# A top-k attention and GELU kernel: two weight units converted ahead of the first slot, and a reordered start

## The chip, the cores and the metric

The kernel runs on one NeuronCore of a Trainium2 chip. The core has five engines that run side by side, each with its own queue in order: TensorE (PE, matrix products), VectorE (DVE), ScalarE (ACT), GpSimd (POOL) and SyncE (SP, which here only issues transfers). The metric is the time of one execution on the device in microseconds (us), the median of several runs.

## The reference

Attention over 8 batches and 8 heads, 576 rows of 64, in which each row of scores keeps its 32 largest values; then a two-layer MLP with an exact GELU over the 4608 resulting rows of 512.

```python
scores = scale * np.matmul(q, k.transpose(0, 1, 3, 2))        # (8, 8, 576, 576)
kth = np.partition(scores, -32, axis=-1)[..., -32:-31]
scores = np.where(scores >= kth, scores, -1e9)
attn = np.exp(scores - scores.max(-1, keepdims=True))
attn = attn / (attn.sum(-1, keepdims=True) + 1e-09)
x = np.matmul(attn, v)  # heads joined: (4608, 512)
h = x @ w_in            # (4608, 2048)
g = 0.5 * h * (1.0 + erf(h / sqrt(2)))
out = g @ w_out         # (4608, 512)
```

q, k and v arrive as 4-byte floats, w_in and w_out as 8-byte floats. The kernel computes in 4-byte floats, so the weights have to be converted on the chip.

## The kernel before

**Attention.** Two heads of a batch form a pair (32 pairs). Their 576 rows are cut into four blocks of 128 and a rest of 64; the rests of two pairs make one item. There are 144 items, in an order that takes, in the first batch, blocks 0 and 1 of all four pairs first (items 0 to 7), then blocks 2 and 3. For a pair, PE transposes q and k in three pieces (`transpose_qk`, L220), and ACT (for the very first pair partly DVE) copies them out of PSUM. For an item, `scores` (L263) multiplies into two PSUM tiles, `s_ps` (one buffer) and `t_ps` (two buffers under the tag `tp`, shared with all transposes), and ACT evicts them, scaled, in L281 and L282 (L303 and L304 for rests). `top_k` (L309) finds the 32nd value of each row on DVE with eight MAX8 and six MATCH_REPLACE8 per item. `threshold` (L334) is two small POOL instructions. `softmax` (L358) is two ACT instructions per head; `add_small` (L352, POOL) and `inverse` (L346, DVE, L350) make the reciprocal of its sum; `normalise` (L369, L376) multiplies by it, one instruction per head, on POOL or DVE. `transposes` (L384) and `attend` (L426, products L444) give 256 columns of x.

**The MLP.** `l1_piece` (L496) and `l2_piece` (L532) are blocks of products, in a fixed list; `mlp(n)` takes up to n from it, as long as the rows of x that they need are there. GELU runs on ACT (L507), after a load of its table.

**The slots.** The loop at L617 runs over n, one slot per item; everything is put into each engine's queue in the order in which it is written. Slot n holds, in this order: the POOL part of a weight unit (`weights_add`), scores of item n + 2, the product of x for item n - 3, pieces of the MLP, the transposes of item n - 2, the softmax of item n - 1, the q and k transposes of a pair to come, top-k of item n (with `inverse(n - 1)` at its end on DVE), the threshold of item n, `normalise(n - 1)`, the ACT part of the next slot's unit (`weights_size`), the loads of the unit two slots on (`load_weights`), and in the first slots a load of v. Item 7 (`HASTE`) is different: its normalisation is put into the middle of the next top-k, on DVE, so that the MLP can begin in slot 9. The load of the q and k of a later pair is issued by SP when the last piece of a pair has been transposed.

**The weights.** They are cut into 16 units of 256 rows by 512 columns. A unit's 8-byte words are loaded by SP in two transfers (L160), to a part of `w_out_sb` that isn't yet in use, or to an extra tile `words`. ACT makes parts of the result with three instructions (L175, L177, L179; for units of slot 9 and later, `on_pool`, POOL does the third, L191), and POOL adds them up in two (L194, L195). Unit number i of `ORDER` has slot i + 1 (the last one i + 2), so slots 1 to 15 and 17. In a slot before one with a unit, `normalise` has one of its two instructions on DVE, or both if that unit is `on_pool`; without a unit both are on POOL.

**The start.** Memsets on POOL clear the rest blocks of the tiles for k and q, DVE that of the first v tile; POOL makes the identity matrix for the transposes. k of pair 0 is loaded by ACT's queue and its last 64 rows by POOL's; q and everything else by SP's. 16 products of zeros (L596, `WARM`) keep PE occupied until k is there. Then come the transposes of pair 0, the scores of items 0 and 1, and the transposes of pair 1, all ahead of slot 0.

Of the kernel before, what the change touches and what calls it, by code (L numbers as in the profile page):

```python
# [14 lines left out]
def kernel(  # L15
# [19 lines left out]
    nc = tc.nc  # L35
# [34 lines left out]

    raws = {n: [const.tile([P, NJ, 2, D], f32, name=f"raw_{n}{i}") for i in range(m)]
            for n, m in (("k", 2), ("q", 2), ("v", NP + 1))}
    for n, ts in raws.items():
        for t in ts[: 1 if n == "v" else 2]:
            (nc.vector if n == "v" else nc.gpsimd).memset(t[:, NM], 0.0)
    make_identity(nc, ident)
    for t in raws["v"][1:]:
        nc.gpsimd.memset(t[:, NM], 0.0)


    n_pairs = B * NP
# [5 lines left out]
    def load(n, pair, queue=None, queue2=None):  # L87
        if pair >= n_pairs:
            return
        queue = queue or nc.sync  # L90
        queue2 = queue2 or queue
        b, h0 = pair // NP, 2 * (pair % NP)
        t, src = raw_of(n, pair), sources[n]
        for e in range(2):
            queue.dma_start(
                out=t[:, 0:NM, e, :], in_=src[b, h0 + e, 0:SM].rearrange("(t p) d -> p t d", p=P)
            )
            queue2.dma_start(out=t[e * TL : (e + 1) * TL, NM, e, :], in_=src[b, h0 + e, SM:S])

# [18 lines left out]


    ORDER = [0, 1, 2, 3, 8, 9, 4, 5, 10, 11, 6, 7, 12, 13, 14, 15]
    FIRST = 1
    START = 2 * NP + 1
    HASTE = 2 * NP - 1
    WARM = 16
    words = {}
    low = const.tile([P, 1], f32, name="low")
    nc.gpsimd.memset(low, -EXP0 * 2.0**19)
# [1 line left out]
    nc.gpsimd.memset(high, EXP0 * 2.0**-21)  # L131


    SLOT_OF = {u: FIRST + i + (i == UNITS - 1) for i, u in enumerate(ORDER)}
    UNIT_IN = {n: u for u, n in SLOT_OF.items()}
    unit_in = UNIT_IN.get

    def load_weights(n, queue=None):

        queue = queue or nc.sync  # L140
        u = unit_in(n)
        if u is None:
            return
        src, r, c, dst = weights_of(u)
        if src.dtype == f32:
            for x in range(2):
                queue.dma_start(
                    out=dst[:, x], in_=src[(r + x) * P : (r + x + 1) * P, c : c + WS]
                )
            return  # L150


        half, i = src.bitcast(u16), ORDER.index(u)
        if i not in (12, 14, 15):
            at = FT // 2 + 4 * (i % 2)
            t = w_out_sb[:, at : at + 4, :].rearrange("p (a b) n -> p a (b n)", a=2)
        else:
            t = stage.tile([P, 2, 2 * WS], f32, tag="words", name="words")
        for a in range(2):
            queue.dma_start(  # L160
                out=t[:, a].bitcast(u16)[:, 0 : 4 * WS - 1],
                in_=half[(r + a) * P : (r + a + 1) * P, 4 * c + 1 : 4 * (c + WS)],
            )
        words[u] = t
# [16 lines left out]
    def on_pool(u):  # L181

        return SLOT_OF[u] >= START

    made = set()

    def weights_add(u):
        if u in words:
            w, _, below, d = parts(u)
            if on_pool(u):  # L190
                nc.gpsimd.tensor_scalar(  # L191
                    w.bitcast(i32), w.bitcast(u32), 2.0**-13, None, op0=ALU.mult
                )
            nc.gpsimd.tensor_tensor(d, d, below, op=ALU.add)  # L194
            nc.gpsimd.tensor_tensor(d, d, w.bitcast(i32), op=ALU.add)  # L195
        made.add(u)
# [53 lines left out]
    def spread(t, step, n):  # L250

        return bass.AP(tensor=t.tensor, offset=t.offset, ap=[list(t.ap[0]), [step, 2], [1, n]])
# [10 lines left out]
    def scores(i):  # L263
        if i >= N:
            return
        pair, t = items[i]
        S_of[i] = s = work.tile([P, 2 * S], f32, tag="s", bufs=5, name="s")
        s_ps = ps.tile([P, 2, 512], f32, tag="s", bufs=1, name="s_ps")
        t_ps = ps.tile([P, 512], f32, tag="tp", name="t_ps")
        if t < NM:  # L270
            qk = qk_of[pair]
            lhsT = qk[:, t * P : (t + 1) * P]
            nc.tensor.matmul(t_ps[:, 0:P], lhsT=lhsT, rhs=qk[:, SM + P : KT], start=True, stop=True)  # L273
            for c in range(2):
                for e in range(2):
                    rows = slice(e * D, (e + 1) * D)
                    nc.tensor.matmul(  # L277
                        s_ps[:, e, c * 256 : (c + 1) * 256], lhsT=lhsT[rows, :],
                        rhs=qk[rows, KT + c * 256 : KT + (c + 1) * 256], start=True, stop=True,
                    )  # L280
            nc.scalar.activation(spread(s, S + TL, SM), s_ps, func=AF.Copy, scale=scale)  # L281
            nc.scalar.activation(s[:, SM : S + TL], t_ps[:, 0:P], func=AF.Copy, scale=scale)  # L282
        else:
            for r in range(2):
                qk = qk_of[pair + r]
                for e in range(2):
                    nc.tensor.matmul(  # L287
                        t_ps[half(r, e), r * TL : (r + 1) * TL],
                        lhsT=qk[:, SM + e * TL : SM + (e + 1) * TL],
                        rhs=qk[:, SM + P + e * TL : SM + P + (e + 1) * TL],  # L290
                        start=True, stop=True,
                    )

            for r in range(2):
                qk = qk_of[pair + r]
                for e in range(2):
                    rows = slice(e * D, (e + 1) * D)
                    nc.tensor.matmul(  # L298
                        s_ps[half(r, e), r, :], lhsT=qk[rows, SM + e * TL : SM + (e + 1) * TL],
                        rhs=qk[rows, KT:], start=True, stop=True,  # L300
                    )
            s2 = s.rearrange("p (r n) -> p r n", r=2)
            nc.scalar.activation(s2[:, :, 0:SM], s_ps, func=AF.Copy, scale=scale)  # L303
            nc.scalar.activation(  # L304
                s2[:, :, SM:S], t_ps[:, 0:P].rearrange("p (r n) -> p r n", r=2),
                func=AF.Copy, scale=scale,
            )
# [274 lines left out]
    staging = ExitStack()  # L582
    stage = staging.enter_context(tc.tile_pool(name="stage", bufs=1))

    load("k", 0, nc.scalar, nc.gpsimd)
    load("q", 0)
    load("k", 1)
    load("q", 1)
    for n in range(2):
        load_weights(FIRST + n)  # L590


    idle = raws["v"][0][:, NM].rearrange("p e d -> p (e d)")
# [3 lines left out]
    for pair in range(2):  # L597
        for piece in transpose_qk(pair, pair == 0):
            piece()
        if pair == 0:  # L600
            scores(0)
            scores(1)

# [11 lines left out]
    for n in range(ahead):  # L617

        left[0] = 7 if START < n < START + 2 * NP else 8
        weights_add(unit_in(n))  # L620
        scores(n + 2)

        product = attend(HASTE) if n - 2 == HASTE else n - 3 != HASTE and attend(n - 3)
        late = n > START
        mlp(1)
        tr = transposes(n - 2) if n - 2 != HASTE else []
        if product and n > START and done[0] < len(pieces) and pieces[done[0]][0] > ready[0]:

            for piece in tr[:1]:
                piece()  # L630
            tr, ready[0] = tr[1:], n_tok[0]
        softmax(n - 1, 0)
        mlp(1)
        if not late:
            softmax(n - 1, 1)
        mlp(1)
        prep = prep_in.pop(n, [])
        if len(prep) > 1 and len(tr) == 3:
            tr, prep = tr[:1] + prep[:1] + tr[1:], prep[1:]
        for piece in tr[:-1]:  # L640
            piece()
            ready[0] = n_tok[0]
            mlp(1)
        ready[0] = n_tok[0]
        if late:
            softmax(n - 1, 1)
        if n - 1 != HASTE:
            add_small(n - 1)
        for piece in tr[-1:] + prep:
            piece()  # L650
            mlp(1)

        run_gelus()
        mlp(left[0])
        run_gelus()
        if n - 1 == HASTE:

            def hasty():
                st = stat_of[HASTE]
                nc.vector.tensor_scalar(st["den"], st["den"], 1e-9, None, op0=ALU.add)  # L660
                inverse(HASTE)
                normalise(HASTE, 2)

            top_k(n, {1: hasty})
            for piece in transposes(HASTE):
                piece()
        elif n < N:
            top_k(n, {3: lambda: inverse(n - 1)})
        else:
            inverse(n - 1)  # L670
        threshold(n)
        u = unit_in(n + 1)

        if n - 1 != HASTE:
            normalise(n - 1, 0 if u not in words else 2 if on_pool(u) else 1)

        weights_size(unit_in(n + 1))
        if n >= FIRST:
            load_weights(n + 2)
        if n <= NP:  # L680
            load("v", n)

# [37 lines left out]
```

## Time and profile before

| | |
|---|---|
| median of 4 runs | 1652.29 us (1651.49 to 1652.75) |
| the profiled execution: time | 1651.49 us |
| its span, first to last instruction | 1649.7 us |
| mean granted clock of PE | 0.979 |
| busy: PE, DVE, ACT, POOL | 1591.3, 1420.7, 1183.5, 651.2 us |
| first top-k instruction on DVE | 11.59 us after the start of the span |
| first product of the MLP (L496) | 109.1 us |
| bytes moved | 56.14 MB |

The span starts with the first instruction and ends with the last; the time of the run is a little longer. Busy times of the engines overlap. A line of the profile that names a group of instructions has the line of the kernel, the engine, the operation, output and inputs, how many there were, the busy time and the mean of one, and then how long the engine stood idle before them and what released it. Where a line says `PE tp L413 <- ACT s L304`, PE's instruction of line 413 waited for ACT's of line 304. The granted clock is the share of full speed at which TensorE was allowed to run.

### The profile page before, as it was taken

What the parts mean: (1) busy time and instruction counts of PE and PEld (TensorE: products, weight loads), DVE (VectorE), ACT (ScalarE), POOL (GpSimd) and SP (SyncE); (2) the same over time, 40 slices, a digit from 0 to 9 for tenths busy, and PEclk for the clock granted to TensorE, in tenths of its full rate; (3) what the DMA queues carried; (4) which work ended last, traced back from release to release, by engine and by line L of the source; (5) the groups of instructions that cost most, each with busy time, mean ns of one, the idle gap of its engine ahead of it and who ended that gap; (6) DMA issues with size and microseconds to landing.
All of it is one profiled execution on the core that took longest, in us unless ns stands there. A gap on an engine that the chain in (4) does not pass through costs nothing.

```text
span 1649.7 us, 25054 instructions
## 1 busy us (share of the span) xinstructions
PE 1591.3 (96%) x8832; PEld 1078.9 (65%) x8832; DVE 1420.7 (86%) x3051; ACT 1183.5 (72%) x2130; POOL 651.2 (39%) x755
## 2 busy tenths in 40 slices
PE   5679799999999999999999999999999999999999
PEld 4355576766666667676666667676666666666665
DVE  7999899988899889998989988998889888999800
ACT  6889867777777777777777777777777777777720
POOL 3778633333333333333333333333333333333300
PEclk7789899999999999999999999999999999999999
DMA  6424210011101111011100111001110001000000
GB/s 174 140 90 131 55 43 1 14 29 33 46 1 28 30 30 28 1 28 36 30 28 5 38 30 43 1 14 28 44 35 1 27 16 35 2 13 6 2 13 13
DMA packets 126621, 56.14 MB, mean 34 GB/s; under 512 B 117760, under 2 KB 117792, under 8 KB 126496
## 3 DMA queue, kind: packets, MB, share of 16 engines
q1 hardware_dynamic: 125376, 54.25, 12.3%
q8 instruction: 70, 1.15, 0.3%
q14 instruction: 55, 0.45, 0.1%
q10 hardware_dynamic: 1056, 0.26, 0.1%
q0 software_dynamic: 64, 0.03, 0.0%
HBM read 45.08 MB, written 9.44 MB: 33 GB/s over the span
## 4 chain that ended last, share of the span: by engine, by line
PE 92%; ACT 4%; DVE 3%; issue 1%; POOL 0%; ACTq 0%; POOLq 0%
PE h_ps L496 30%; PE y_ps L532 30%; PE o L444 9%; PE s_ps L277 8%; PE tp L413 7%; PE tp_qk L232 2%; DVE top L324 2%; PE t_ps L273 2%; DVE rest L327 1%; PE o L455 1%; PE s_ps L298 1%; PE tp_t L395 1%; ACT s L364 1%; ACT s L363 1%; PE t_ps L287 0%
## 5 line engine op out<-in xcount | busy, mean ns | idle before, releaser
L324 DVE MAX8 top<-rest 128x8 f32<-128x576 f32 x864 | 609.3, 747 | 0.0
L496 PE MATMUL h_ps<-xT,w_in_sb 128*128 128x256 f32 (+1 forms) x2560 | 553.8, 361 | 3.8 <-ACT g L507 3.8
L532 PE MATMUL y_ps<-w_out_sb,g 128*128 128x512 f32 x1152 | 549.4, 599 | 0.0
L496 PEld LDWEIGHTS h_ps<-xT,w_in_sb 128*128 128x128 f32 x2560 | 429.5, 191 | 67.4 <-issue 19.7
L376 POOL TENSOR_SCALAR s<-s,rden 128x576 f32<-128x576 f32 x265 | 454.3, 1723 | 0.4 <-DVE rden L350 0.4
L327 DVE MATCH_REPLACE8 rest<-top,rest 128x576 f32<-128x576 f32 x576 | 423.3, 742 | 0.0
L356 POOL TENSOR_SCALAR den<-den 128x2 f32<-128x2 f32 x143 | 31.7, 222 | 832.5 <-ACT s L364 831.9
L532 PEld LDWEIGHTS y_ps<-w_out_sb,g 128*128 128x128 f32 x1152 | 195.0, 190 | 166.1 <-issue 164.9
L281 ACT ACTIVATE s<-s_ps 128x1024 f32<-128x1024 f32 x128 | 131.5, 1028 | 168.1 <-PE s_ps L277 146.3
L364 ACT ACTIVATE s<-s,bias 128x576 f32<-128x576 f32 x288 | 223.3, 775 | 12.7
L363 ACT ACTIVATE s<-s,neg 128x576 f32<-128x576 f32 x288 | 224.1, 778 | 0.3 <-POOL neg L339 0.2
L413 PEld LDWEIGHTS tp<-ident,s 128*128 128x128 f32 x1152 | 146.6, 145 | 116.0 <-issue 58.9
L420 ACT COPY pt<-tp 128x512 f32<-128x512 f32 x256 | 147.1, 574 | 102.7 <-PE tp L413 102.6
L327 DVE MATCH_REPLACE8 rest<-top,s 128x576 f32<-128x576 f32 x288 | 211.7, 742 | 0.0
L413 PE MATMUL tp<-ident,s 128*128 128x128 f32 x1152 | 180.0, 281 | 27.8 <-ACT pt L396 20.0
L324 DVE MAX8 top<-s 128x8 f32<-128x576 f32 x288 | 201.8, 742 | 3.9 <-ACT s L282 3.9
L444 PE MATMUL o<-pt,raw_v 128*64 128x256 f32 x1280 | 155.8, 391 | 0.0
L277 PE MATMUL s_ps<-qk 64*128 64x256 f32 x1024 | 151.5, 416 | 0.7 <-ACT s L281 0.7
L350 DVE RECIPROCAL rden<-den 128x2 f32<-128x2 f32 x144 | 23.0, 160 | 138.2 <-POOL den L356 137.9
L444 PEld LDWEIGHTS o<-pt,raw_v 128*64 128x64 f32 x1280 | 87.8, 139 | 66.5 <-issue 24.6
L277 PEld LDWEIGHTS s_ps<-qk 64*128 64x128 f32 x1024 | 91.6, 193 | 23.5 <-issue 1.6
L507 ACT ACTIVATE g<-h_ps 128x512 f32<-128x512 f32 x144 | 78.6, 595 | 33.7 <-PE h_ps L496 32.9
(67 smaller groups left out, 1088.3 us busy)
## 6 DMA issues: line engine op xcount, KB each, us to landing
raw_q<-in_q_dram SPq DMA_DIRECT2D x64, 128.0 KB, 2.4
raw_v<-in_v_dram SPq DMA_DIRECT2D x64, 128.0 KB, 2.5
out_dram<-y SPq DMA_DIRECT2D x32, 256.0 KB, 2.2
w_out_sb<-in_moe_w_in_dram SPq DMA_DIRECT2D x16, 511.8 KB, 4.9
raw_k<-in_k_dram SPq DMA_DIRECT2D x62, 128.0 KB, 2.5
w_out_sb<-in_moe_w_out_dram SPq DMA_DIRECT2D x10, 511.8 KB, 4.1
words<-in_moe_w_out_dram SPq DMA_DIRECT2D x6, 511.8 KB, 4.5
raw_q<-in_q_dram SPq DMA_DIRECT2D x64, 16.0 KB, 2.2
```

The source lines that it names most:

```text
L277: nc.tensor.matmul(s_ps[:, e, c * 256 : (c + 1) * 256], lhsT=lhsT[rows, :], rhs=qk[rows, KT + c * 256 : KT + (c + 1) * 256], start=True, s ...
L281: nc.scalar.activation(spread(s, S + TL, SM), s_ps, func=AF.Copy, scale=scale)
L324: nc.vector.max(st["top"][:, e, 8 * r : 8 * r + 8], cur[e])
L327: nc.vector.match_replace(rest[:, e], st["top"][:, e, 8 * r : 8 * r + 8], cur[e], LOWEST)
L363: nc.scalar.activation(s, s, func=AF.Prelu, bias=st["neg"][:, e, 1:2], scale=1.0, alpha=STEEP)
L364: nc.scalar.activation(s, s, func=AF.Exp, bias=st["bias"][:, e : e + 1], scale=1.0, accum_out=st["den"][:, e : e + 1],)
L376: (nc.vector if e >= 2 - on_dve else nc.gpsimd).tensor_scalar(s, s, st["rden"][:, e : e + 1], None, op0=ALU.mult)
L413: nc.tensor.transpose(tp[:, j * P : (j + 1) * P], s[:, first + j * P : first + (j + 1) * P], ident)
L420: nc.scalar.copy(out=dst, in_=tp.rearrange("p (j n) -> p j n", j=NM))
L444: nc.tensor.matmul(o[e * D : (e + 1) * D, 0:n], lhsT=vt[:, j, e, :], rhs=pt[:, e * NM + j if j < NM else 2 * NM, :], start=(j == 0), stop= ...
L496: nc.tensor.matmul(h_tile(u)[:, i, :], lhsT=w_in_sb[:, ko, f * P : (f + 1) * P], rhs=xT[:, ko, c0 : c0 + n], start=(ko == 0), stop=(ko == ...
L532: nc.tensor.matmul(y_of[sub], lhsT=g_of[u][:, i, sub * P : (sub + 1) * P], rhs=w_out_sb[:, f, :], start=(f == 0), stop=(f == FT - 1),)
```

## The change

1. The first two units have slot 0: their ACT part is put ahead of the loop, behind the transposes of pair 1. All later units move two slots ahead, to slots 1 to 13 and 15. Three units instead of two are loaded ahead of the loop, and the third one's words go to the extra tile.
2. The memsets are redistributed: POOL clears only the first k tile, DVE the others. The loads of pair 0 are issued ahead of the identity matrix, so POOL issues k's last rows as its second task.
3. Nine products of zeros in place of 16.
4. The scores of item 0 are evicted in three instructions: ACT takes the first head's 512 columns, DVE the 128 of the rest and the second head's 512.

What follows from 1: the number of units that are `on_pool` goes from eight to six, and slots 13 and 16 have no unit's ACT part any more, so their `normalise` is on POOL.

```diff
-    for n, ts in raws.items():
-        for t in ts[: 1 if n == "v" else 2]:
-            (nc.vector if n == "v" else nc.gpsimd).memset(t[:, NM], 0.0)
-    make_identity(nc, ident)
-    for t in raws["v"][1:]:
-        nc.gpsimd.memset(t[:, NM], 0.0)
+    nc.gpsimd.memset(raws["k"][0][:, NM], 0.0)
+    for t in raws["v"][:1] + raws["q"] + raws["k"][1:] + raws["v"][1:]:
+        nc.vector.memset(t[:, NM], 0.0)
...
+    load("k", 0, nc.scalar, nc.gpsimd)
+    load("q", 0)
+    make_identity(nc, ident)
...
-    WARM = 16
+    WARM = 9
...
-    SLOT_OF = {u: FIRST + i + (i == UNITS - 1) for i, u in enumerate(ORDER)}
+    SLOT_OF = {u: max(0, i - 1) + (i == UNITS - 1) for i, u in enumerate(ORDER)}
+    def units_in(n):
+        return [u for u in ORDER if SLOT_OF[u] == n]
...
-        if i not in (12, 14, 15):
+        if i not in (2, 12, 14, 15):
...
+            if i == 0:
+                nc.scalar.activation(s[:, 0:SM], s_ps[:, 0], func=AF.Copy, scale=scale)
+                nc.vector.tensor_scalar(s[:, SM : S + TL], t_ps[:, 0:P], scale, None, op0=ALU.mult)
+                nc.vector.tensor_scalar(s[:, S + TL :], s_ps[:, 1], scale, None, op0=ALU.mult)
+                return
...
-    load("k", 0, nc.scalar, nc.gpsimd)
-    load("q", 0)
     load("k", 1)
     load("q", 1)
-    for n in range(2):
-        load_weights(FIRST + n)
+    for u in units_in(0) + units_in(1):
+        load_weights(u)
...
+    for u in units_in(0):
+        weights_size(u)
...
-        weights_add(unit_in(n))
+        for u in units_in(n):
+            weights_add(u)
...
-            normalise(n - 1, 0 if u not in words else 2 if on_pool(u) else 1)
-
-        weights_size(unit_in(n + 1))
-        if n >= FIRST:
-            load_weights(n + 2)
+            normalise(n - 1, 0 if not us else 2 if on_pool(us[0]) else 1)
+        for u in us:
+            weights_size(u)
+        for u in units_in(n + 2):
+            load_weights(u)
```

More of the change, by code (lines that the diff above doesn't have):

```diff
@@ L122 @@
     ORDER = [0, 1, 2, 3, 8, 9, 4, 5, 10, 11, 6, 7, 12, 13, 14, 15]
-    FIRST = 1
     START = 2 * NP + 1
     HASTE = 2 * NP - 1
-    WARM = 16
+    WARM = 9
     words = {}
@@ L131, with load_weights @@
     nc.gpsimd.memset(high, EXP0 * 2.0**-21)
-    SLOT_OF = {u: FIRST + i + (i == UNITS - 1) for i, u in enumerate(ORDER)}
[L135 to L143, printed above, removed]
+    SLOT_OF = {u: max(0, i - 1) + (i == UNITS - 1) for i, u in enumerate(ORDER)}
+    def units_in(n):
+        return [u for u in ORDER if SLOT_OF[u] == n]
+    def load_weights(u):
+        queue = nc.sync
         src, r, c, dst = weights_of(u)
@@ L671 @@
         threshold(n)
-        u = unit_in(n + 1)
+        us = units_in(n + 1)
         if n - 1 != HASTE:
-            normalise(n - 1, 0 if u not in words else 2 if on_pool(u) else 1)
-        weights_size(unit_in(n + 1))
-        if n >= FIRST:
-            load_weights(n + 2)
+            normalise(n - 1, 0 if not us else 2 if on_pool(us[0]) else 1)
[3 more added lines that the diff above has]
+            load_weights(u)
         if n <= NP:
```

## The prediction, made before the changed kernel was run

> **What bounds the kernel now.** I read the page first (busy shares by slice), then stretches of the first 240 us, then who waited for whom in them, and last the order of time on ScalarE (ACT) in the first 35 us. "Slot n" is round n of the main loop; T is the time from the start of the span.
>
> The page: TensorE (PE) is busy nearly always, except in the first four of the 40 slices (41 us each) and a little in the fifth. The two lines below are the busy tenths of PE and its granted clock.
>
> ```profile
> PE 1591.3 (96%) x8832; PEld 1078.9 (65%) x8832; DVE 1420.7 (86%) x3051; ACT 1183.5 (72%) x2130; POOL 651.2 (39%) x755
> PE   5679799999999999999999999999999999999999
> ...
> PEclk7789899999999999999999999999999999999999
> ```
>
> The stretches say where PE's time is lost (columns: stretch, length, busy us of each engine, granted clock, DMA share, GB/s). From 240 on PE never pauses before the tail; from 20 to 100 VectorE (DVE) is full and ACT nearly.
>
> ```profile
> 30.00:40.00 10.00, 6.15 (x25) 4.10 (x23) 9.96 (x23) 8.88 (x16) 7.20 (x6) 0.50 0.64 170
> ...
> 80.00:90.00 10.00, 3.96 (x21) 2.74 (x22) 9.89 (x23) 9.54 (x18) 7.50 (x7) 0.79 0.33 105
> ...
> 160.00:170.00 10.00, 7.34 (x27) 4.65 (x26) 8.91 (x19) 6.60 (x12) 6.90 (x3) 0.89 0.36 120
> ...
> 190.00:200.00 10.00, 4.44 (x34) 2.33 (x32) 9.01 (x20) 9.00 (x14) 5.14 (x5) 0.92 0.26 60
> 200.00:210.00 10.00, 8.06 (x40) 5.06 (x41) 8.99 (x20) 6.55 (x13) 7.70 (x7) 0.57 0.00 0
> ...
> 240.00:400.00 160.00, 160.00 (x930) 109.69 (x928) 146.61 (x316) 117.63 (x215) 60.70 (x76) 1.00 0.07 17
> ```
>
> So the end is set by two things: when the first product of the MLP (h_ps, T 109.1) can start, and PE's pauses between that and T 206. Everything PE does later follows without a gap, so a microsecond lost or won there is one at the end.
>
> The waits: between T 20 and 100 DVE waited 0.4 us in all, for ACT, and ACT waited only for PE, never for DVE. After T 100 PE's pauses are ACT's doing; the largest is 4.6 us in slot 16/17.
>
> ```profile
> DVE den L660 <- ACT s L364: 0.4, 1, 0.4
> ...
> ACT pt L420 <- PE tp L413: 3.7, 7, 0.7
> ACT xT L449 <- PE o L444: 2.9, 2, 1.8
> ACT qk L236 <- PE tp_qk L232: 1.6, 2, 1.3
> ...
> PE tp L413 <- ACT s L304: 4.6, 1, 4.6
> ...
> PE h_ps L496 <- ACT g L507: 2.7, 1, 2.7
> ```
>
> The reader should see that from T 20 ACT is a chain of its own (with PE round trips) that runs as fast as DVE: if ACT is made late early on, nothing gives the time back.
>
> In the order of time on ACT: unit 0's conversion, L175+L177+L179, from 20.28 to 23.7, then scores, then the first softmax.
>
> ```profile
> 20.28 1.23 ACT L175 ACTIVATE w_in_sb<-w_out_sb,low 128x1024 int32<-128x1024 int16 x1
> ...
> 23.73 1.01 ACT L281 ACTIVATE s<-s_ps 128x1024 f32<-128x1024 f32 x1
> ...
> 24.79 0.78 ACT L363 ACTIVATE s<-s,neg 128x576 f32<-128x576 f32 x1
> ...
> 30.89 0.14 DVE L350 RECIPROCAL rden<-den 128x2 f32<-128x2 f32 x1
> ```
>
> **The change, part by part.** *The start.* Nine products instead of 16: the 32 passes took 5.17 us from 1.04; by the stretches 18 passes are done at about 4.0. PE then waits for k. Its two main loads were issued on ACT's queue at 0.7 and 1.2 and land 3.5 us later (median), so at 4.8 instead of PE's start at 6.05: -1.25. k's last rows are issued by POOL at about 1.0 instead of 2.73 and land 2.8 us later, before they are needed; the identity moves behind these two issues (1.26 us) and is ready near 2.9 instead of 1.87, covered by the 4.8; if it weren't, the start would move by the difference. Eight memsets move to or stay on DVE (0.17 each, 1.4 us); DVE is idle until 6.69. SP's first short load waits for one of them (POOL's before), no later than now. The first scores: ACT took 1.02 and 0.27, from 10.37 to 11.56. Now ACT evicts 512 columns (0.58, as L420) beside DVE's 512 (0.69, its own L236 row, an upper bound; 0.41 for 256 columns is the lower) and its 128 before them, while PE still multiplies. That is -0.5. First top-k: 11.59 - 1.75 = 9.85. The same 1.7 holds for the second scores, which wait for that eviction, and the copies of pair 1: ACT is free at 15.62 - 1.7 = 13.9.
>
> *Two units in slot 0.* One conversion takes ACT 3.42 (28.73 to 32.14). Units 0 and 1 run from 13.9 to 20.75 (their loads, issued from 7.83, land after 5.1 to 7.5 us, just in time), scores(2) to 21.95. Then ACT needs the copy of pair 2's k. PE had those rows at 19.13; now the third unit's two loads (1.02 MB) go ahead of them on SP's queue, 2.9 us at the 0.36 MB/us of T 12 to 16: 22.0, transposes at half clock 1.1, copy 23.2 to 23.8 (bounds for this wait: 0, if the rows are in time, and 2.9). The third unit to 27.2, scores(3) 1.06, softmax(0) 3.21: 31.5 against 28.1 now, **+3.4** (6.85 of work, 3.0 of idle time at 15.6 and 18.5 filled, 1.7 by the start, 1.3 by the rows). DVE ends item 1 at 30.89 - 1.75 = 29.15 and waits for this softmax's sum until about 31.9: the gain of the start is gone.
>
> Queued behind it: POOL's adds of two units (4 of 2.45 from 16.3) end at 26.1 and threshold(0) waits behind them until 26.5; ACT asks for it at 28.3, so 1.8 us of cover. Unit 2's adds end at 31.4, level with the softmax. SP's load for slot 2 waits for unit 1's adds (26.1), and pair 0's v (now at 23.1) behind it; v is first read at 52.85.
>
> *Carried on.* In slots 1 to 8 ACT has as many conversions as before (one a slot, three operations up to n = 7). Its gaps there are the PE round trips of the waits above, which move with it. The sum lies ready some 1.4 to 2.6 us before DVE asks for it in slots 1 to 7 (slot 1: 28.4 against 30.89), and in slot 8 DVE already waits 0.4; a lag of 3.4 uses that up. So the first MLP product is late by +3.4. Bounds: +2.0 (k's rows in time, PE's clock higher in the round trips) and +5.5 (cold start, below).
>
> *The end of the conversions.* The ACT parts of the last three units move from slots 13, 14 and 16 to 11, 12 and 14, so slots 13 and 16 have none left. In slot 16 L175 and L177 (196.31 to 198.7, 2.4 us) stand before the eviction L303/L304 for which PE waits 4.6 us: **-2.4**. What is late next is item 15's normalisation: no unit follows, so POOL does it (2 of 1.72, to about 197.65) instead of DVE (0.95); L304 would now end at 197.5, so the two meet. In slot 13 PE was not waiting for ACT (0), but item 12's normalisation on POOL ends near 162.4 where PE wants it at 162.2: **+0.3**. The half clock after that pause lasts from 198.4 to 208.7; with a pause of 2.6 us in place of 4.6 PE would still pause again for 2 us, and I take no change; bounds -1.7 (one of its three parts of 3.4 us gone, and PE twice as fast in it) and +1.
>
> *Units 8 and 9 of the order* stand in slots 7 and 8 instead of 9 and 10 and so get ACT's third operation; but by slot the operations are the same, so nothing.
>
> Sum: +3.4 - 2.4 + 0.3 = +1.3. The profiled run took 1651.5 (span 1649.7, 1.8 around it), 0.8 below the median of four; against the median this is 1652.3 + 1.3 = 1653.6.
>
> [...] The row: in this run the passes went from 7 a microsecond to 7 in half of one at about 4.0, that is 2.9 us after the first product, and the half clock later lasted 10.2 us (0.61 of the clock in 198 to 200, 0.83 in 208 to 210). [...]
>
> **Rivals.** *Slower: a cold start.* If PE stays at half clock after nine products, four transposes take 1.11 instead of 0.66 (twice), two t_ps 0.80 for 0.49 and eight s_ps 2.08 for 1.13: 2.2 us with the first scores. That eats the -1.25 and delays ACT's 13.9 alike: +1.3 + 2.2 = +3.5, 1655.8, and with k's rows late by the whole 2.9 1657.4. It decides when the clock is granted later than about 5 us. For it: the products end at 4.0, right at the change of rate. Against: 0.8 us of pause is short.
>
> *Faster: the lag is absorbed.* If pair 2's k is in time (-1.3), and ACT's round trips (8.2 us in all, above) shrink by 2 because PE is at full clock oftener (0.72 each where it is at half, 0.26 at full), the start costs +0.1; with a third of the half clock gone the sum is 0.1 - 2.4 + 0.3 - 1.7 = -3.7, and with all three (-3.4 in PE's work from 203 to 208.7 and before) -5.4: 1648.6 to 1646.9. It decides from a start of +0.5 down. For it: ACT's and DVE's paces differ by 0.1 us a slot only. Against: the SP queue is in order, and the pauses in slot 17 stay.
>
> *No effect:* conversions ahead gate nothing, since the MLP's order and start don't depend on them; then only the start counts: -1.75, 1650.5. Against: ACT's queue has no room before T 20.
>
> **How the numbers follow.** Likeliest, 0.45: lag and relief nearly cancel, 1653.6, own range 1651 to 1656.5. Cold start or late rows 0.25, lag absorbed 0.22, only the start 0.08. Measurements here tell 0.2% (3.3 us, 1649.0 and 1655.6) from no change. Likeliest: 0.07 slower, 0.36 same, 0.02 faster; cold 0.20 slower, 0.05 same; absorbed 0.18 faster, 0.04 same; start alone 0.03 faster, 0.05 same. Together 0.23 faster, 0.50 same, 0.27 slower. The range, 1646.5 to 1658.5, takes in both outer rivals' mid values.
>
> **What would show it.** First top-k near 9.9; ACT's first conversion near 13.9; DVE waiting 2 to 3 us for the softmax's sum at the first L350; h_ps starting at 111 to 113; PE's pause near T 200 about 2.6 us instead of 4.6. I am wrong if DVE doesn't wait there, if the first k transposes take 1.1 us, or if PE gains new pauses after T 110.

## The result and the profile after

The changed kernel takes 1654.25 us (median; 1652.76 to 1656.87), the kernel before 1652.02 (1649.72 to 1653.03) in the same comparison: 1.0014 times as long, 95% interval 1.0010 to 1.0019. That is 2.2 us more, inside the 0.2% that counts as no change here, and 0.65 above the predicted 1653.6. The profiled run took 1654.05 with a span of 1652.3; before 1651.49 and 1649.7. So the span grew by 2.6 where the sum said 1.3. The interval leaves out 1, so the changed kernel is a little slower, by less than what counts as a change.

The page first: total, and the tenths of PE and its clock.

```profile
PE 1592.2 (96%) x8818; PEld 1077.8 (65%) x8818; DVE 1420.2 (86%) x3056; ACT 1184.9 (72%) x2131; POOL 650.9 (39%) x750
PE   5679799999999999999999999999999999999999
...
PEclk7689999999999999999999999999999999999999
```

Busy times are the same to 1.4 us: nothing was saved or added, only moved. The stretches of the kernel after show where:

```profile
30.00:40.00 10.00, 4.39 (x15) 2.58 (x15) 7.09 (x16) 8.90 (x14) 9.60 (x8) 0.50 0.93 254
80.00:90.00 10.00, 3.77 (x26) 2.13 (x22) 9.89 (x23) 9.02 (x15) 6.92 (x7) 0.98 0.30 106
...
160.00:170.00 10.00, 8.01 (x49) 3.62 (x47) 10.00 (x22) 4.94 (x9) 4.99 (x6) 1.00 0.56 165
190.00:200.00 10.00, 9.01 (x52) 4.57 (x47) 9.12 (x20) 6.34 (x13) 3.51 (x6) 1.00 0.06 14
200.00:210.00 10.00, 5.79 (x31) 3.93 (x29) 10.00 (x24) 8.79 (x16) 4.21 (x6) 0.66 0.20 45
240.00:400.00 160.00, 160.00 (x933) 110.67 (x932) 145.79 (x314) 116.02 (x213) 60.79 (x75) 1.00 0.07 18
```

DVE (third busy number) lost 2.9 us in 30 to 40, where it had been full and is 7.09 now. From 240 on PE is full in both, so the end again follows what comes before it.

The start of the kernel after, in order of time ("..." marks lines left out, here and below):

```profile
1.04 3.80 PE L599 MATMUL warm<-raw_v 128*128 128x128 f32 x18 [1.04 <-DVE raw_v L75]
5.51 0.63 PE L231 MATMUL tp_qk<-ident,raw_k 128*128 128x128 f32 x4 [0.67 <-DMA raw_k<-in_k_dram]
...
9.85 0.60 ACT L282 ACTIVATE s<-s_ps 128x512 f32<-128x512 f32 x1 [1.65 <-PE s_ps L276]
10.48 0.69 DVE L284 TENSOR_SCALAR s<-s_ps 128x512 f32<-128x512 f32 x1 [1.41 <-ACT s L282]
11.09 1.41 DVE L329 MAX8 top<-s 128x8 f32<-128x576 f32 x2
```

The first top-k begins at 11.09, half a microsecond before the old 11.59. DVE's eviction of the second head didn't run beside ACT's, but behind it. In the middle, on ACT, DVE and POOL:

```profile
15.30 1.25 ACT L174 ACTIVATE w_in_sb<-w_out_sb,low 128x1024 int32<-128x1024 int16 x1
...
18.77 1.23 ACT L174 ACTIVATE w_in_sb<-w_out_sb,low 128x1024 int32<-128x1024 int16 x1
...
22.19 1.00 ACT L286 ACTIVATE s<-s_ps 128x1024 f32<-128x1024 f32 x1
...
23.25 0.58 ACT L235 COPY qk<-tp_qk 128x512 f32<-128x512 f32 x1
...
23.72 1.25 ACT L174 ACTIVATE w_in_sb<-words,low 128x1024 int32<-128x1024 int16 x1
...
30.62 2.38 POOL L194 TENSOR_TENSOR w_in_sb<-w_in_sb,words 128x1024 int32<-128x1024 int32 x1
...
33.20 1.24 ACT L174 ACTIVATE w_in_sb<-w_out_sb,low 128x1024 int32<-128x1024 int16 x1 [0.94 <-DMA w_out_sb<-in_moe_w_in_dram]
...
33.34 0.17 DVE L355 RECIPROCAL rden<-den 128x2 f32<-128x2 f32 x1 [2.88 <-POOL den L361]
```

Three conversions (15.30, 18.77, 23.72) stand before the first softmax where there was one. It ends at 31.43 (before 28.0). DVE waits 2.88 for its sum: POOL makes it only behind its adds of the third unit, which end at 33.0. Then PE: the first product of the MLP and the instructions behind its main pauses.

```profile
113.06 7.07 PE L501 MATMUL h_ps<-xT,w_in_sb 128*128 128x256 f32 x32
...
166.77 0.33 PE L400 MATMUL tp_t<-ident,s 128*128 128x128 f32 x1 [0.39 <-POOL s L381]
...
170.97 1.57 PE L501 MATMUL h_ps<-xT,w_in_sb 128*128 128x256 f32 x4 [2.57 <-ACT g L512]
...
177.39 0.45 PE L292 MATMUL t_ps<-qk 128*64 128x64 f32 x8 [0.79 <-ACT pt L425]
...
198.84 0.45 PE L292 MATMUL t_ps<-qk 128*64 128x64 f32 x8 [0.99 <-ACT pt L425]
...
202.69 0.48 PE L400 MATMUL tp_t<-ident,s 128*128 128x128 f32 x1 [2.37 <-POOL s L381]
...
205.86 1.12 PE L418 MATMUL tp<-ident,s 128*128 128x128 f32 x4 [1.84 <-ACT pt L401]
...
212.53 0.30 PE L405 MATMUL tp_t<-ident,s 128*64 128x128 f32 x1 [0.69 <-POOL s L381]
```

Set against the same instructions of before, PE is late by 4.0 at 113.06, 4.5 at 170.97, 5.25 at 177.39 and 198.84; by 3.05 behind the pause of 2.37 (it was 4.58); by 2.9 at 205.86, by 1.7 at the end of the half clock (211.54), and by 2.6 behind the last new pause. The 2.6 stay to the end.

### The profile page after: what moved, and what is told of

It is laid out like the page before. It is cut to its first block, busy times and chain, and to the rows that moved or that the text cites. A ratio compares the mean times of both kernels' runs of the same rounds, so it can differ in the third digit from the quotient of the medians.

```text
span 1652.3 us, 25026 instructions
## 1 busy us (share of the span) xinstructions
PE 1592.2 (96%) x8818; PEld 1077.8 (65%) x8818; DVE 1420.2 (86%) x3056; ACT 1184.9 (72%) x2131; POOL 650.9 (39%) x750
## 4 chain that ended last, share of the span: by engine, by line
PE 89%; DVE 5%; ACT 3%; POOL 1%; DMA 1%; issue 0%; ACTq 0%; SPq 0%; POOLq 0%; DVEq 0%
PE y_ps L537 30%; PE h_ps L501 29%; PE o L449 8%; PE s_ps L276 8%; PE tp L418 7%; DVE top L329 3%; DVE rest L332 2%; PE tp_qk L231 2%; PE t_ps L272 2%; PE o L460 1%; PE tp_t L400 1%; PE s_ps L303 1%; ACT s L369 1%; POOL s L381 1%; ACT s L368 1%
## 5 line engine op out<-in xcount | busy, mean ns | idle before, releaser
L381 POOL TENSOR_SCALAR s<-s,rden 128x576 f32<-128x576 f32 x269 | 461.1, 1723 | 0.8 <-issue 0.4
L286 ACT ACTIVATE s<-s_ps 128x1024 f32<-128x1024 f32 x127 | 130.5, 1027 | 165.7 <-PE s_ps L276 144.0
```

The lines of the kernel that those rows point to most:

```text
L381: (nc.vector if e >= 2 - on_dve else nc.gpsimd).tensor_scalar(s, s, st["rden"][:, e : e + 1], None, op0=ALU.mult)
```

## The experiments

**Which part costs.** e1 keeps the new start and puts the units back to their old slots; e2 is the kernel before with the units alone moved; e3 is the changed kernel with the units one slot ahead of before instead of two. In e1 and e3 the loads move along, and the third unit's words go where the kernel before puts them.

```diff
 e1, in the changed kernel
-    SLOT_OF = {u: max(0, i - 1) + (i == UNITS - 1) for i, u in enumerate(ORDER)}
+    SLOT_OF = {u: 1 + i + (i == UNITS - 1) for i, u in enumerate(ORDER)}
...
 e2, in the kernel before (the loops over units_in as in the change)
-    SLOT_OF = {u: FIRST + i + (i == UNITS - 1) for i, u in enumerate(ORDER)}
+    SLOT_OF = {u: max(0, i - 1) + (i == UNITS - 1) for i, u in enumerate(ORDER)}
...
 e3, in the changed kernel
-    SLOT_OF = {u: max(0, i - 1) + (i == UNITS - 1) for i, u in enumerate(ORDER)}
+    SLOT_OF = {u: i + (i == UNITS - 1) for i, u in enumerate(ORDER)}
```

> The changed kernel with the units of weights in their old slots (1 to 15 and 17), so only the start is changed. Lag theory (the loss comes from ACT being made late by the units of slot 0): nothing delays ACT, so the 0.5 us won at the first top-k (11.1 instead of 11.6) is kept: first MLP product at 108.6 instead of 109.1, pause near T 200 still 4.6 us, time 0.5 us under the kernel before (0 to -1). Start theory (fewer products of zeros and the new order of the first loads cost time): 1 us or more above the kernel before.

> The kernel before with only the units moved: two in slot 0, the others two slots ahead. Lag theory: ACT begins the first unit at about 15.6, first MLP product at 113.0 to 113.6, pause near T 200 2.4 instead of 4.6 us, time 2 to 3 us above the kernel before. Start theory: within 0.5 us of the kernel before.

> The changed kernel with one unit in slot 0 and the others one slot ahead (slots 0 to 14 and 16). Lag theory: 3.4 us less work for ACT ahead of slot 0 than in the changed kernel, so that about 3.0 us of idle time nearly hold it: first MLP product at 109.1 to 110, while slot 16 still has no ACT part of a unit, pause near T 200 about 2.4 us: 1 to 2 us under the kernel before, 3 to 4 under the changed one. Rival (the loss lies in the late slots, in the normalisations that POOL gets): slots 14 and 16 have those here, so no faster than the kernel before.

e1: 1651.83, ratio 0.9998 (0.9989 to 1.0007). e2: 1654.81, 1.0018 (1.0009 to 1.0027). e3: 1648.85, 0.9982 (0.9973 to 0.9991). Against the kernel before of that comparison (1652.06) the two halves are -0.2 and +2.8, which add up to +2.5, about the +2.2 of the changed kernel. The start gave nothing that stands clear of its interval, where 0.5 was expected: in e1 the first top-k came at 10.95, but ACT's first conversion at 20.38 (before 20.28), since ACT waited 2.43 for the product of scores(2) in front of it (before 1.65) and 1.00 for pair 2's k (1.32); the MLP started at 109.94, not at the 108.6 expected. In e2 it started at 114.71, later than expected (113.0 to 113.6); its profiled run took 1656.49, the slowest of the eleven. In e3:

```profile
15.26 1.27 ACT L174 ACTIVATE w_in_sb<-w_out_sb,low 128x1024 int32<-128x1024 int16 x1
...
20.57 1.23 ACT L174 ACTIVATE w_in_sb<-w_out_sb,low 128x1024 int32<-128x1024 int16 x1
...
28.98 1.23 ACT L174 ACTIVATE w_in_sb<-w_out_sb,low 128x1024 int32<-128x1024 int16 x1
...
30.34 0.14 DVE L355 RECIPROCAL rden<-den 128x2 f32<-128x2 f32 x1
...
109.00 7.07 PE L501 MATMUL h_ps<-xT,w_in_sb 128*128 128x256 f32 x32
```

One conversion more than before, from 15.26 to 18.75, lies where ACT was idle; softmax(0) ends at 28.25, DVE doesn't wait, and the MLP starts at 109.00 as before (109.08). The relief near T 200 is there all the same: PE's pause is 2.36 in e3, and 4.58 in e1 with the old slots. So the first unit ahead is free, and the second costs at the MLP's start the whole of its conversion and 0.6 more. e3 is faster than both kernels, with intervals that don't meet the changed kernel's; against the kernel before its 0.18% is, like the 0.14% the other way, inside what counts as no change.

**What the lag is made of.** My theory was ACT's work: three conversions stand before softmax(0) where one stood. The rival: the rows of pair 2, the words of the units or POOL's adds would hold the first slots anyway. With two units in slot 0, e4 takes 2.5 us of ACT's work away, e5 puts the third unit's loads behind the rows of pair 2, and e6 does both.

```diff
 e4: in weights_size, for units 0 and 1 only
-        nc.scalar.activation(d, first, func=AF.Relu, bias=low, scale=2.0**19)
+        if not less:
+            nc.scalar.activation(d, first, func=AF.Relu, bias=low, scale=2.0**19)
...
 e5
-    for u in units_in(0) + units_in(1):
+    for u in units_in(0):
         load_weights(u)
...
             scores(1)
+            for u in units_in(1):
+                load_weights(u)
```

> The changed kernel without the first ACT instruction (L174, 1.23 us) of units 0 and 1; their target is cleared by POOL instead, early, so these two units of weights are wrong. Lag theory: ACT has 2.5 us less to do ahead of slot 0 and carries that to the end: first MLP product at 110.6 instead of 113.1, time 2.4 us under the changed kernel, level with the kernel before. Rival (what is late in slot 1 is POOL's adds or the transfers, ACT only waits for them): first MLP product and time move by less than 1 us.

> The changed kernel with the two loads of the third unit (1 MB) moved behind the loads of q and k of pair 2 on SP's queue. In the changed kernel ACT is free for the copy of that k at 23.3 and PE has it ready 0.45 us earlier, so the rows are not what ACT waits for: first MLP product at 112.5 to 113.1, time within 0.7 us of the changed kernel. Transfer theory (the rows that come late are what makes ACT late): first MLP product 1 us or more earlier.

> The run without L174 of units 0 and 1 (again these units of weights are wrong), and with the third unit's loads behind pair 2's q and k. In the run without L174 alone ACT stood 2.5 us waiting for the copy of pair 2's k, where before it worked, so the 2.5 us taken from it came to nothing. Two-bounds theory (ACT's work and the rows of pair 2's k end at nearly the same time, so that only both together free the start): with both, the first softmax ends near 29 instead of 31.4, first MLP product at 110.3 to 111, time 1.5 to 2.5 us under the changed kernel. If something else holds slot 1 (POOL's adds), it stays at 112.5 or more.

e4: 1653.44, ratio 1.0008 (1.0000 to 1.0017); e5: 1653.82, 1.0011 (1.0002 to 1.0019); e6: 1653.67, 1.0008 (0.9999 to 1.0017). None brings the lag down: the MLP starts at 112.89, 113.67 and 113.05. So my theory failed in e4 (it said 110.6), and the rival held. The times, +1.4, +1.5 and +1.4 against the kernel before, lie under the changed kernel's +2.2, but the intervals overlap. In e4 and e6 ACT's 2.5 us came back as idle time; e5 made nothing better by itself. Its MLP is late because its start was: in that run the eight products of the first scores took 2.08 instead of 1.13, and ACT's first conversion began at 16.33. In e4 (its line numbers are 2 higher) ACT had to wait with the copy of pair 2's k, whose rows are behind the third unit:

```profile
21.86 1.08 PE L233 MATMUL tp_qk<-ident,raw_k 128*128 128x128 f32 x4 [5.13 <-DMA raw_k<-in_k_dram]
...
22.98 0.58 ACT L237 COPY qk<-tp_qk 128x512 f32<-128x512 f32 x1 [2.48 <-PE tp_qk L233]
```

In e6, with the rows early, ACT waited for the third unit's words, now late, and for those of the fourth:

```profile
22.91 1.24 ACT L176 ACTIVATE w_in_sb<-words,low 128x1024 int32<-128x1024 int16 x1 [1.67 <-DMA words<-in_moe_w_in_dram]
32.67 1.23 ACT L176 ACTIVATE w_in_sb<-w_out_sb,low 128x1024 int32<-128x1024 int16 x1 [1.22 <-DMA w_out_sb<-in_moe_w_in_dram]
```

The idea of two bounds, work and rows, fell with this. The fourth unit's words go to the place of the second's; SP issues that load only when POOL has added the second unit up (27.73 in the kernel after), which made POOL's adds a further suspect. Three more kernels took those away: e9 without the third unit, e10 without POOL's adds of the first two, e11 both.

```diff
 e9
+        if u == ORDER[2]:
+            nc.gpsimd.memset(dst, 0.0)
+            return
...
 e10
-        if u in words:
+        if u in words and u not in ORDER[:2]:
```

> The changed kernel without the third unit (no load, no ACT part, no adds; its place in w_in_sb is cleared by POOL, so one unit of w_in counts as zero). Theory of several bounds, each ending near the other: the sixth of the conversions before slot 1 is gone (-3.4 on ACT, which was 23.7 to 27.2), pair 2's rows come 2 to 3 earlier, so softmax(0) ends at 28.3 and DVE waits at most 0.5 there; but the load of the fourth unit goes to the second unit's words and is issued only behind POOL's adds of that unit (27.7), so ACT waits for it from about 29.1 to 33.2 and is no earlier than before from there: h_ps at 112 to 113.3, time within 1 us of the changed kernel (1653.3 to 1655.2). Rival, ACT's work alone sets the lag: h_ps at 109.6, time 1651.

> The changed kernel without POOL's four adds of the first two units (their sums are left out, so two units of w_in are wrong). Theory of several bounds: the load of the fourth unit is issued at about 24.8 instead of 27.7 and ACT's 0.94 of waiting for it goes; the third unit's adds still follow its conversion, 27.3 to 32.1, so the sum is ready at about 32.3 instead of 33.1 and DVE waits about 2.0; h_ps at 112.1 (-0.9), time 1653.3. Rival, POOL's adds are the bound in slots 0 and 1: DVE's wait is 1 or less, h_ps 111 or less, time 1652 or less.

> Both at once: without the third unit and without POOL's adds of the first two. Theory of several bounds: with ACT's work, the transfers and POOL's adds all taken away, softmax(0) ends at 28.3, the fourth unit's words lie ready when ACT comes to them at 29.1, and the shift of 4 against the kernel before is gone: h_ps at 109 to 110, time 1650 to 1651.5. If h_ps stays at 112 or more, something else holds slots 0 to 3 and the cause of the lag is open.

e9: 1654.41, ratio 1.0015 (1.0006 to 1.0024); e10: 1652.89, 1.0004 (0.9995 to 1.0013); e11: 1652.20, 1.0002 (0.9994 to 1.0011). e10 came as the theory of several bounds had it: the wait for the fourth unit gone, DVE's wait 1.34 (expected 2.0), the MLP at 112.35. e9 kept the time of the changed kernel, with the fourth unit converted at 33.11, but softmax(0) ended at 31.05 and not at 28.3, and the MLP started at 114.36, 1.1 later than expected. e11 missed too: 111.79 and not 109 to 110, 1652.20 and not 1650 to 1651.5. Both mainly for one reason (in e9 ACT also waited 0.5 for POOL's threshold), shown by ACT's order of time in e11 (its L289, L290 and L177 are L286, L287 and L174 of the changed kernel):

```profile
22.29 1.00 ACT L289 ACTIVATE s<-s_ps 128x1024 f32<-128x1024 f32 x1
...
26.36 1.02 ACT L289 ACTIVATE s<-s_ps 128x1024 f32<-128x1024 f32 x1 [2.43 <-PE s_ps L279]
...
31.37 1.25 ACT L177 ACTIVATE w_in_sb<-w_out_sb,low 128x1024 int32<-128x1024 int16 x1
```

and by PE's between the two evictions:

```profile
23.50 0.80 PE L275 MATMUL t_ps<-qk 128*128 128x128 f32 x2 [3.81 <-ACT s L290]
24.23 2.08 PE L279 MATMUL s_ps<-qk 64*128 64x256 f32 x8
```

Scores(3) can't be multiplied before scores(2) are out of PSUM, and these stand behind both conversions of slot 0 in ACT's queue, at 22.2. PE, idle until then, multiplies at half rate (2.08 for what took 1.13 at T 16). In the changed kernel the third unit's conversion covers this round trip; without it ACT waits 2.43. In e3 the second conversion stands behind scores(2), and PE's round trip runs beside it: there, with two conversions ahead of it as in e11, softmax(0) ends at 28.25 and not at 30.64.

**The start.** e7 is e3 with the second head's first scores in a PSUM tile of their own, e8 is e3 with the normalisation of slots 14 and 16 on DVE, e12 is the changed kernel with 16 products of zeros.

```diff
 e7, in e3
+            if i == 0:
+                s_of[1] = ps.tile([P, DM], f32, tag="l2", name="s2_ps")
...
-                nc.vector.tensor_scalar(s[:, S + TL :], s_ps[:, 1], scale, None, op0=ALU.mult)
+                nc.vector.tensor_scalar(s[:, S + TL :], s_of[1], scale, None, op0=ALU.mult)
...
 e8, in e3
-            normalise(n - 1, 0 if not us else 2 if on_pool(us[0]) else 1)
+            normalise(n - 1, 2 if n in (14, 16) else 0 if not us else 2 if on_pool(us[0]) else 1)
...
 e12, in the changed kernel
-    WARM = 9
+    WARM = 16
```

> One unit in slot 0, and the second head's first scores in a PSUM tile of their own. In the changed kernel DVE's half of the eviction began only after ACT's half had ended (10.48, ACT's to 10.45), so the split won nothing; if that is because both halves are read from one tile, DVE now begins with ACT, near 9.85, first top-k at 10.4 instead of 11.0, and time 0.3 to 0.6 us under the run with one unit. If it has another cause, no change.

> One unit in slot 0, with the normalisations of slots 14 and 16 on DVE as the kernel before has them. PE's pause of 2.4 us near T 197 ends with POOL's second normalisation (197.1); ACT's L309, which PE also needs there, ends at 197.2, so nothing is won in slot 16, and 0 to 0.4 us in slot 14. If POOL's normalisation were the cause of that pause it would fall to 1.5 us or less, and time by 1 us.

> The changed kernel with 16 products of zeros instead of nine, all else the same. The products end at 5.9 to 7 (32 passes from 1.04, 18 of them by 4.8, the rest at 7 to 14 in a microsecond), so the transposes of k start 0.4 to 1.4 later, the first top-k at 11.5 to 12.4. Theory, ACT's chain from its first conversion sets the end: the conversion starts that much later and h_ps with it (113.4 to 114.4), time 1654.5 to 1655.7. Rival, PE at full clock earlier makes up for it or the transfers hold the chain anyway: h_ps 113.1 and time as the changed kernel within 0.4.

e7: 1649.27, ratio 0.9981 (0.9972 to 0.9990), no different from e3. With a tile of its own DVE's half starts with ACT's (9.72):

```profile
9.76 0.69 DVE L287 TENSOR_SCALAR s<-s_ps 128x512 f32<-128x512 f32 x1 [0.81 <-PE s_ps L279]
10.37 1.41 DVE L332 MAX8 top<-s 128x8 f32<-128x576 f32 x2
```

The top-k is 0.67 earlier than in e3 and ACT's first conversion 0.81 (14.45), yet the MLP starts at 109.56, no earlier than e3's 109.00: ACT gave the 0.8 back waiting for PE's transposes of q and k (1.3 in 20 to 100, e3 0.3) and for x (2.9, e3 2.1). So the expected 0.3 to 0.6 of time didn't come.

e8: 1650.44, 0.9990 (0.9981 to 0.9998). The pause near T 200 is hardly smaller, and now ACT's:

```profile
199.02 0.66 PE L418 MATMUL tp<-ident,s 128*128 128x128 f32 x4 [2.24 <-ACT s L309]
...
209.89 0.30 PE L405 MATMUL tp_t<-ident,s 128*64 128x128 f32 x1 [1.23 <-POOL s L381]
```

In time e8 is no better than e3 (-1.9 against -3.2 in their own comparisons; the intervals overlap). Its MLP started at 110.48 and e3's at 109.00, though the two kernels are the same up to slot 14: in e8 ACT stood 0.9 for a transfer before its conversion at 30.03. So one trace's start of the MLP is good to about 1.5 us, and smaller steps between kernels (as in e7, e10, e11 and e12) aren't shown by it alone.

e12: 1655.33, 1.0019 (1.0010 to 1.0028), so +3.2 against the kernel before, where the changed kernel has +2.2. The products ended at 6.6, the first conversion began at 16.25 (+0.95), the MLP at 113.61 (+0.55), all inside the expected bounds. By the medians seven products fewer are worth about 1 us with two units in slot 0, where ACT's chain has no slack left at its start; the intervals overlap, and e5, with nine products, began its first conversion as late, so this is likely and not shown.

**The sum that holds.** These are ACT's first conversion, its waits from 20 to 100 (from the waits view, each to 0.1) and the start of the MLP:

| kernel | first conversion | ACT's waits | h_ps |
|---|---|---|---|
| after | 15.30 | 7.2 | 113.06 |
| e2, old start | 16.42 | 7.8 | 114.71 |
| e3, one unit | 15.26 | 6.5 | 109.00 |
| e4, less ACT work | 15.0 | 9.8 | 112.89 |
| e5, late unit | 16.33 | 6.8 | 113.67 |
| e6, both | 15.26 | 9.8 | 113.05 |
| e7, one unit, two tiles | 14.45 | 7.8 | 109.56 |
| e8, one unit, DVE | 15.27 | 7.8 | 110.48 |
| e9, no third unit | 15.26 | 11.8 | 114.36 |
| e10, no adds | 15.77 | 6.2 | 112.35 |
| e11, neither | 15.43 | 9.2 | 111.79 |
| e12, 16 products | 16.25 | 6.8 | 113.61 |

Against the kernel after, the change of the start, of ACT's work (-3.5 where a conversion is gone, -2.5 for the two instructions of e4 and e6) and of the waits add up to that of h_ps in every row, within 0.35. In e11: +0.1 - 3.5 + 2.0 = -1.4, measured -1.3. In e6: 0 - 2.5 + 2.6 = +0.1, measured 0. In e9: 0 - 3.5 + 4.6 = +1.1, measured +1.3. So ACT's chain accounts for the start of the MLP, but with two units in slot 0 most of what is taken from its work comes back as waits for PE, for rows or for words. The sum is bookkeeping, with the waits of each kernel's own trace: it says where the time went, and doesn't forecast it.

## Why the prediction was right, and where its terms were off

The direction, the place (the first softmax) and the size came out, and of the three terms each was there. The sum for the span was +1.3 against 2.6 measured, and the pieces were less good than the total; that the start's miss (+1.25) was just the wait for rows that fell away (-1.3) was chance. Of the signs named, DVE's wait (2.88), the MLP's start (113.06, at the edge) and PE's pause (2.37) came; the first top-k (11.09 for 9.9) and the first conversion (15.30 for 13.9) didn't.

*The start, -1.75, was -0.5.* Its two parts failed apart. The products: they ended at 4.84, not at 4.0, since I had added up counts that take in a pass twice when it lies in two stretches; in the kernel before the eighteenth pass began at 4.38. That cost nothing, because k's transposes began at 5.51, not 4.8: PE had to wait 0.67 for k's rows, which landed later than the median I took. That is -0.54, not -1.25. The eviction on two engines, -0.5, was 0: from the first transpose to the first top-k it took 5.54 before and 5.58 after, because DVE's read of the tile waits for ACT's (the trace names L282 as what released it). e7, with two tiles and no such wait, shows that it is the shared tile; whether the chip or the program's own ordering of reads of a tile makes the wait, no run separates.

*The wait for pair 2's k, +1.3, was 0,* and the later start took its place. The rows came as forecast (transposes at 21.69, forecast 22.0), but the conversions ran to 22.2 instead of 20.75, so that ACT found k ready at 23.25. The forecast had ACT wait for that copy until 23.2, so a later start only ate up the wait; that it was late by just as much is chance, and softmax(0) ended at 31.43 (forecast 31.5).

*The lag at the first MLP product, +3.4, was +4.0,* 113.06 where 111 to 113 was named. Missing was the fourth unit. I had written that SP's load waits for POOL's adds of unit 1, and followed only pair 0's v behind it; the load itself was late (issued at 27.73), and ACT stood 0.94 for it. e10 takes that wait away: 112.35, though its first conversion began 0.5 later. POOL's adds of the third unit ended at 33.0, not "level with the softmax" at 31.4, so DVE's wait was 2.88 from a later moment, 30.46 (forecast 2.7 from 29.15).

*The relief, -2.4, was -2.2.* ACT's eviction ended at 202.76 and POOL's normalisation at 202.63: the two meet as forecast, and e8, which speeds up one of them, shortens PE's pause by 0.1 only.

*Item 12 on POOL, +0.3:* PE waited 0.39 at 166.77.

*No change from the half clock* was wrong. Near T 200 it lasted 6.8 us instead of 10.2 (202.2 to 209.1, before 198.4 to 208.7): one of its three parts went, the case that I had priced at -1.7 and left out. It gave -1.2 (from +2.9 at 205.86 to +1.7 at 211.54). The shorter pause isn't enough of a reason: e2, e3 and e6 have the same pause of 2.36 or 2.37 and kept 10.2 us (e3's clock was 0.79 in 190 to 200 and 0.70 in 200 to 210; in e2 and e6 it is an estimate from the times of PE's products). Two new pauses of PE that no term held took the gain back and more: 0.79 at 177.39, with a half clock that fell on 171.5 to 174.9 instead of 167.7 to 171.1 (+0.75 together), and 0.69 at 212.53, for POOL's normalisation (+0.9). New pauses after T 110 were named as a sign of being wrong, and here the prediction was; the total hides it, since the three come to +0.5 together. Which pauses appeared went with where the half clock fell in e3 and e7: e3, without one near 170 (four products of h_ps at 167.70 took 1.03), pauses for 1.61 at 171.86, and e7, nearly the same kernel, with one from about 168.2 on (1.91 for four at 168.40), doesn't. No experiment was made on that.

*The rivals.* A cold start didn't happen in the profiled run: 15 of the 18 passes ran at the slow rate (0.213 us apart), but the four transposes took 0.63. In e10 and e11 they took 1.09, with the first top-k at 11.55 and 11.21, and in e5 the first scores were slow, with the first top-k at 12.11: a slow start is there in some runs, and their first top-k is 0.1 to 1.0 us later than the 11.09 here, not 2.2. The absorbed lag was e3's case, by another cause than the rows or the clock: one unit more is absorbed, two are not. That the change does nothing but the start is refuted by e1 and e2.

## What to carry to other kernels

Work moved ahead is free only as far as the engine that takes it is idle there: count the idle time in front of the move (3.0 us here) against one piece of it (3.5), and try the half move. Here it is worth 3.2 us where the whole one costs 2.2. When a cause seems to be one engine's work, ask what is ready at the moment when that work is gone; each of ACT's conversions covered a row, a round trip or a load that took its place. In these kernels a PSUM tile read by two engines wasn't read by both at once (10.48 behind 9.85, with two tiles 9.76 beside 9.72); here an eviction was split only by giving each engine its own tile, and even that didn't show in the time.

## What the runs showed of the hardware

PE's products of zeros start at 1.04 or 1.05 in every run, but the moment at which their rate rises is another in each. Below are stretches of one microsecond for these products alone (columns: stretch, length, PE busy and count, weight loads, granted clock, DMA share, GB/s; a count takes in the passes that lie only partly in the stretch), first for e12, then for e2, with the same 32 passes:

```profile
3.00:4.00 1.00, 1.00 (x7) 1.00 (x7) 1.00 0.80 182
4.00:5.00 1.00, 1.00 (x7) 1.00 (x7) 1.00 0.92 208
5.00:6.00 1.00, 1.00 (x11) 1.00 (x10) 1.00 0.72 163
```

```profile
3.00:4.00 1.00, 1.00 (x7) 1.00 (x7) 1.00 1.05 237
4.00:5.00 1.00, 1.00 (x6) 1.00 (x6) 1.00 0.91 206
5.00:6.00 1.00, 1.00 (x8) 1.00 (x7) 1.00 0.65 147
6.00:7.00 1.00, 1.00 (x10) 0.92 (x9) 1.00 0.33 75
```

Pass by pass, behind the first one they start 0.213 us apart, and 0.111 later on. The rate rose at 3.9 in the kernel before, at 4.8 in e12 and at 5.75 in e2; the 32 passes took 5.17, 5.60 and 6.07. The column of the granted clock reads 1.00 all the while: in the traces before and after the first entry of the clock is its first rise to full speed, at 3.88 and 4.26, so ahead of it the passes tell the rate and the column doesn't. I had read 4.0 as a property of the kernel, and it was one run's chance: of the eleven traces with nine products, k's first four transposes took 0.63 in seven, 0.87 and 0.93 in one each, and 1.09 in two. In the three kernels with 32 passes the change moved by 1.9 us, from 3.9 to 5.75, with the first pass at 1.04 in each.

The later half clock: in the traces before and after, the stretches of one clock between its first rise and its rise near T 209 last 3.41, 6.83, 10.24, 13.65, 20.48, 27.31, 30.72, 40.96 or 61.44 us, each a whole multiple of 3.41. Near T 200 the half clock lasted from 198.4 to 208.7 before (10.24, three times 3.41), and from 202.2 to 209.1 after (6.83, two). With PE's shorter pause of 2.2 to 2.4 us, the 20 products of x behind it took 2.38 to 2.97 in nine kernels and 3.73, 3.47 and 3.44 in e2, e3 and e6 (3.47 before); by my estimate from these times the nine had two, the others three, and what decides it stays open.
